# Memory attention and a bilinear layer: seven block products for every quarter from batch 1 on

## The chip, the cores and the metric

The kernel runs on one core of one Trainium2 chip. The metric is the device time of one launch in microseconds (us). Before the change it is 511.87 us, the median of three runs (511.76 to 512.64).

The engines are called as in the profile: PE is the matrix engine (TensorE), DVE is VectorE, ACT is ScalarE, POOL is GpSimd, SP issues the DMAs.

## What is computed

```python
# per batch and head: seq 576, head_dim 64, 32 memories; 8 batches, 8 heads
a = softmax of phi over the sequence
k_m, v_m = a^T k, a^T v                    # 32 x 64 each
attn = softmax(q k_m^T / 8)                # 576 x 32
x = attn v_m                               # all heads side by side: 576 x 512 per batch
# then a layer on x
a, b = x @ w1, x @ w2                      # 512 -> 1024 each
out = ((a * b) @ w3) @ w_out               # 1024 -> 1024 -> 512
```

All is fp32. Nothing between `v_m` and `a * b` is non-linear, so the kernel multiplies `v_m` with w1 and w2 first (a matrix M per batch, 256 x 2048) and then the softmax with M. `w3 @ w_out` is formed once.

## The kernel before

**Numbers.** A matrix is split into a high part, rounded to a short fp32 form (fp32r), and a low part, the rest. A product is three matmuls: high x high, high x low, low x high. Every such matmul has 288 columns, half of a batch's 576 tokens.

**A batch** has three parts.

1. The attention: softmax of phi, the memories (L236, L245), the scores (L285), the second softmax on DVE and ACT, and M in four quarters. A quarter of M (token `M`, L381) is written by PE into two PSUM banks; its high part is a copy on ACT (`Mh`, L392), its low part a subtraction on DVE (`Ml`, L400).
2. a and b. In batches 0 and 1 all four quarters are made *plainly*: `ab_unit` takes 12 matmuls (L655) for 128 features of a and b and half of the tokens, ACT copies a out of PSUM (L664), DVE multiplies it with b (L667). That is 16 units, 192 matmuls a batch. From batch 2 on two of the four quarters are made plainly (96 matmuls) and two by *seven block products* instead of eight (Winograd's form of Strassen's scheme), `block_product` (L695), 6 matmuls each, 84 for the two.
3. The output, also by seven block products (`out_unit`, L782): GpSimd forms sums of g = a * b (L733, L744, L746, L748), ACT and DVE split the operands (`h`, L760; `l`, L766), PE takes 14 units of 12 matmuls, ACT and DVE combine (L799, L807, L815), SP stores.

**Block products of a quarter.** The operands are sums of M's blocks and of the softmax's quarters. Of M: ACT copies one block out of PSUM (`Mr`, L409), DVE forms three sums (`Ms`, L412), ACT rounds them (`Mt`, L420), DVE forms the low parts (`Mu`, L424). Of the softmax: four sums on DVE (`T`, L342) with high and low parts (`Th`, `Tl`, L353). The seven products meet in three pairs of banks, alpha, beta and gamma. ACT copies three intermediate states out of PSUM (L707), DVE adds the banks to them (L717), in six instructions a quarter, and multiplies four times (L727).

**PSUM** is eight banks: four under ab (lent by number), two under o, two under x.

**Order.** Every engine executes its instructions in the order in which a list of tokens emits them: `FIRST` for batch 0, `SECOND` for batch 1, `BATCH` for the rest. A sign says which batch a token is for: `-` the current one, none the next one, `+` the one after. `P1` is a block product, `k`, `e`, `v` its copies, sums and multiplications, `O` an output unit, `f` and `S` GpSimd's sums, `C1` to `C5` the conversion of the float64 weights at the start, `W` the product w3 @ w_out, `K`, `D`, `E`, `F` and the like its splitting, `Q` a difference of weight columns that block products need (L906, DVE).

Of the kernel before, what the change touches and what calls it, by code (L numbers as in the profile page):

```python
# [37 lines left out]
"""
SECOND = """
-mu1 A A tok1 a -tr1 g -M2 a -M3 A -ah1 -Mh3 -Mh2 a A Q -al1 g g a g -Ml3 phi1 A A top a g bm a bs g kv1 exp A A  # L40
phi2 -Ml2 Q f0 a be mem g A norm memc block a h0 g A a tok2 blockc +top M1 a g sc0 +exp g scc0 M0 mx0 A A Mh1 l0 kv2
a f2 g a f1 sb0 ex0 f3 Ml1 A sm0 a Mh0 A g a A g Ml0 +bm g A +norm O mu0 +bs a h1 h2 l1 h3 a l3 l2 tr0 +be sc1 M2
+mem g g M3 Mr Ms O Mh2 S2 S3 scc1 Mt Ml2 mx1 h4 +memc O Mu S1 l4 h6 p1 h5 l5 l6 S4 Mr O O ah0 h8 O h7 Ms u2 C11 l7
O +block h13 h9 l8 sb1 Mt O ex1 h10 Mh3 l9 Mu l10 al0 O p5 O l13 h11 l11 O sm1 O h12 q2 C22 l12 mu1 tr1 Ml3 O
+blockc ah1 O C21 al1 C12
"""
BATCH = """
A A a a g A g a g -T1 h0 phi2 tok2 -T3 A -T2 a g A l0 a -T4 g +top A A -Th1 +bm -Th0 h1 a g +exp A -Tl0 M0 +bs a a
sc0 M1 f0 -Tl1 g Mh0 g Mh1 scc0 Ml0 P1 k10 Ml1 mx0 kvx2 k11 P5 P6 k51 k50 P2 sb0 k20 P3 e10 k21 +be P5 e11 ex0 e20
v1 k50 e21 P7 P1 f2 k51 e40 v2 e41 sm0 k11 v4 k10 P4 l1 P3 P6 P2 e30 v3 k20 e20 k21 f1 f3 e21 P7 mu0 h2 e40 v2 e41 O  # L50
e11 e10 P4 v4 v1 e30 v3 M2 sc1 M3 h3 l2 l3 kvy2 Mh2 Mr +mem Ms S2 +norm h4 +memc O Ml2 S3 p1 l4 h5 Mt tr0 O S1 O h6
S4 scc1 l5 Mu ah0 h8 O l6 Mr h7 O mx1 u2 O l7 C11 h10 O l8 h9 Ms h11 l9 O p5 O l10 l11 h12 sb1 O +block al0 Mt h13
l12 C22 l13 ex1 Mh3 sm1 O Mu mu1 Ml3 +blockc q2 O tr1 ah1 C12 O C21 al1
"""

# [6 lines left out]
def memory_attention__then__bilinear_ffn_kernel(  # L62
# [39 lines left out]
    ps_ab = ctx.enter_context(tc.tile_pool(name="ps_ab", bufs=1, space=bass.MemoryType.PSUM))  # L102
    ps_ox = ctx.enter_context(tc.tile_pool(name="ps_ox", bufs=1, space=bass.MemoryType.PSUM))
# [5 lines left out]
    NQ = 4  # L109
    FQ = DF // NQ  # L110
# [8 lines left out]
    class Banks(list):  # L119
        slots = ()  # L120

        def done(self, i):
            if self.slots:
                free_banks.append(self.slots[i])

    free_banks = [0, 1, 2, 3]

    def pair_ab(n=2):
        slots = [free_banks.pop(0) for _ in range(n)]
        banks = Banks(ps_ab.tile([P, 512], F32, name="ab", tag=f"ab{s}") for s in slots)  # L130
        banks.slots = slots
        return banks

    def pair_o(n=2):
        o = ps_ox.tile([P, 2, 512], F32, name="o")
        return Banks([o[:, i] for i in range(2)] + [o])

    def pair_x(n=2):
        x = ps_ox.tile([P, 2, 512], F32, name="x")
        return Banks([x[:, i] for i in range(2)] + [x])  # L140

    def both(banks):
        return [(slice(0, 2), banks[2])] if banks[2:] else [(slice(i, i + 1), x.unsqueeze(1)) for i, x in enumerate(banks)]
# [41 lines left out]
    ready, beside = {}, {}  # L185

    def attention(b):
# [20 lines left out]
        def spread_max(bank):  # L208
            v["mxb"] = bank(1)
            ps = v["mxb"][0][:, : NT * P]  # L210
            for t in range(NT):
                nc.tensor.transpose(ps[:, t * P : (t + 1) * P], v["mx"][:, t : t + 1].broadcast_to([P, P]), ident)

        def sub_max():
# [8 lines left out]
            v["mxb"].done(0)  # L223
# [4 lines left out]
        def memories(bank):  # L228
            kvt = loaded.pop(("kv", b))
            ps = v["memories"] = bank()  # L230
            if b - 1 in beside:
                ps = v["memories"] = Banks(x[:, HALF : HALF + 2 * D] for x in ps[:2])
# [30 lines left out]
        def blocks(bank):  # L263
            v["blocks"] = bank(1)
            ps = v["blocks"][0][:, : NT * P]
            for t in range(NT):
                nc.tensor.transpose(ps[:, t * P : (t + 1) * P], v["kvm"][:, t], ident)

        def spread():
            ps = v["blocks"][0][:, : NT * P]  # L270
            p4 = ps.rearrange("p (t g m) -> p t g m", t=NT, m=M)
            for t, (ko, vo) in enumerate(((0, D), (D, 0))):
                nc.vector.tensor_scalar_mul(km[b % 2][ko : ko + D], p4[ko : ko + D, t], scale)
                nc.vector.tensor_copy(out=vm[b % 2][vo : vo + D], in_=p4[vo : vo + D, t])
            v["blocks"].done(0)

        def scores(n, bank):
# [3 lines left out]
            banks = v["scores", n] = bank()  # L281
# [21 lines left out]
        def soft_max(n):  # L303
            st = v["st", n] = att.tile([P, NBLK, 1], F32, name=f"st{n}")
            nc.vector.tensor_reduce(out=st, in_=v["s"][:, n], axis=AX.X, op=ALU.max)
# [9 lines left out]
        def soft_sum(n):  # L315
            ss = v["ss", n] = att.tile([P, NBLK, 1], F32, name=f"ss{n}")
# [8 lines left out]
        def probs(n):  # L325
            if n == 0:
                v["at"] = att.tile([P, 2, S], F32, name="at")
            nc.vector.transpose(out=v["at"][:, n], in_=v["s"][:, n].rearrange("p k m -> p (k m)"))

        def probs_high(n):  # L330
            if ("A", b) not in ready:
                ready["A", b] = [att.tile([P, 2, S], F32R, name=x, tag=x) for x in ("ah", "al")]
            nc.scalar.copy(out=ready["A", b][0][:, n], in_=v["at"][:, n])

        def probs_low(n):
            hi, lo = (x[:, n] for x in ready["A", b])
            nc.vector.tensor_tensor(out=lo, in0=v["at"][:, n], in1=hi.bitcast(F32), op=ALU.subtract)

        def prob_sums(i):
            (x11, x21), (x12, x22) = [[v["at"][:, n, t * HALF : (t + 1) * HALF] for t in range(NT)] for n in range(2)]  # L340
            out, in0, in1 = {1: (x11, x12, x11), 3: (x12, x22, x12), 2: (x22, x22, x11), 4: (x21, x21, x22)}[i]
            nc.vector.tensor_tensor(out=out, in0=in0, in1=in1, op=ALU.subtract)  # L342
# [6 lines left out]
        def sums_low(n):  # L349
# [18 lines left out]


    m_tags = (2, 3, 4, 0, 5, 6, 7, 1)  # L370

    def memory_weights(b):
# [3 lines left out]
        def step(q, bank):  # L376
            ps = ms["ps", q] = bank()
# [603 lines left out]
```

## Time and profile before

| | us |
|---|---|
| median of three runs | 511.87 |
| the profiled execution: span from the first to the last instruction | 510.1 |
| PE busy | 500.6 |
| DVE busy | 446.4 |
| ACT busy | 311.5 |
| POOL busy | 147.2 |

What the page gives for the profiled execution's own time is its span; the runs' median stands 1.8 us above it (511.87 - 510.1).

How to read it: the busy time of an engine is the time in which at least one of its instructions runs. Matmuls overlap, so a matmul's own duration is about twice the distance to the next one. DVE's instructions overlap too, by some 0.08 us. The view by stretches gives the busy time of each engine between two times; stretches here are cut where PE starts a batch's a and b (74.06 us for batch 0, then 131.10, 191.91, 245.96, 300.01, 354.07, 408.11, 460.02); PE's last matmul ends near 505.9.

### The profile page before, as it was taken

How to read it: one execution, taken by the hardware profiler on the slowest of the kernel's cores; microseconds unless marked ns; L12 is line 12 of the kernel's file. 1: busy time of each engine (PE TensorE's matmuls, PEld its weight loads, DVE VectorE, ACT ScalarE, POOL GpSimd, SP SyncE). 2: the span in 40 equal slices, each digit the busy share in tenths (PEclk: the TensorE clock that was granted, in tenths of full speed). 3: DMA queues.
4: the chain of work that ended last, by engine and by line, in shares of the span. 5: the costliest groups of instructions: out<-in, count | busy, mean ns of one | idle time of the engine just before them, and what ended most of it. 6: DMA issues, size and time to landing. Idle time of an engine off the chain costs nothing.

```text
span 510.1 us, 11167 instructions
## 1 busy us (share of the span) xinstructions
PE 500.6 (98%) x4416; PEld 434.6 (85%) x4416; DVE 446.4 (88%) x805; ACT 311.5 (61%) x566; POOL 147.2 (29%) x158
## 2 busy tenths in 40 slices
PE   8998999999999999999999999999999999999996
PEld 7344449889889899889988998899898998899996
DVE  4978988888889997999899989999899979997692
ACT  6877889866346655656474747565566555654451
POOL 0003105755020800153023602180108011630480
PEclk9999999999999999999999999999999999999999
DMA  8999943703674047201821064203620230011001
GB/s 282 414 405 350 387 168 110 276 1 118 209 267 154 3 140 243 83 3 41 267 87 73 26 197 161 84 26 128 231 84 3 67 120 1 3 48 48 0 24 69
DMA packets 29795, 68.86 MB, mean 135 GB/s; under 512 B 1840, under 2 KB 10032, under 8 KB 29744
## 3 DMA queue, kind: packets, MB, share of 16 engines
q1 hardware_dynamic: 29744, 68.16, 37.8%
q8 instruction: 34, 0.56, 0.5%
q14 instruction: 17, 0.14, 0.1%
HBM read 58.72 MB, written 9.44 MB: 134 GB/s over the span
## 4 chain that ended last, share of the span: by engine, by line
PE 89%; DMA 7%; ACT 1%; DVE 1%; SPq 1%; issue 0%; ACTq 0%
PE ab L655 25%; PE o L782 19%; PE x L782 11%; PE ab L695 9%; PE ab L782 5%; DMA kv<-in_kv 4%; PE ab L381 3%; PE x L236 3%; DMA raw<-in_w_out 2%; PE o L557 2%; PE x L557 2%; PE x L695 2%; PE o L695 2%; PE o L381 1%; PE x L381 1%; PE ab L285 1%
## 5 line engine op out<-in xcount | busy, mean ns | idle before, releaser
L655 PE MATMUL ab<-ah,mh 128*128 128x288 f32 x320 | 95.8, 300 | 0.0
L655 PE MATMUL ab<-al,mh 128*128 128x288 f32 x320 | 94.4, 295 | 0.0
L655 PE MATMUL ab<-ah,ml 128*128 128x288 f32 x320 | 94.4, 295 | 0.0
L760 ACT CAST sh<-g 128x576 fp32r<-128x576 f32 x98 | 65.7, 676 | 34.6 <-PE x L782 8.5
L766 DVE TENSOR_TENSOR sl<-g,sh 128x576 fp32r<-128x576 f32 x98 | 82.2, 855 | 3.2 <-ACT sh L760 2.6
L733 POOL TENSOR_TENSOR g<-g,g 128x288 f32<-128x288 f32 x32 | 26.2, 838 | 201.0 <-DVE g L667 196.5
L782 PE MATMUL o<-sh,Wh 128*128 128x288 f32 x248 | 73.6, 297 | 0.0
L782 PE MATMUL o<-sh,Wl 128*128 128x288 f32 x248 | 73.2, 295 | 0.0
L782 PE MATMUL o<-sl,Wh 128*128 128x288 f32 x248 | 73.1, 295 | 0.0
L655 PEld LDWEIGHTS ab<-ah,mh 128*128 128x128 f32 x320 | 60.2, 188 | 4.2 <-DVE g L667 1.7
L655 PEld LDWEIGHTS ab<-al,mh 128*128 128x128 f32 x320 | 60.2, 188 | 0.2 <-issue 0.2
L655 PEld LDWEIGHTS ab<-ah,ml 128*128 128x128 f32 x320 | 60.2, 188 | 0.0
L664 ACT COPY a_sb<-ab 128x288 f32<-128x288 f32 x80 | 31.4, 399 | 33.9 <-PE ab L655 33.0
L667 DVE TENSOR_TENSOR g<-ab,a_sb 128x288 f32<-128x288 f32 x80 | 35.6, 453 | 18.4 <-PE ab L655 13.7
L744 POOL TENSOR_TENSOR q<-g,g 128x288 f32<-128x288 f32 x28 | 23.0, 849 | 93.2 <-ACT mh L392 69.2
L782 PEld LDWEIGHTS o<-sh,Wh 128*128 128x128 f32 x248 | 46.6, 188 | 2.9 <-issue 2.5
L782 PEld LDWEIGHTS o<-sh,Wl 128*128 128x128 f32 x248 | 46.6, 188 | 0.0
L782 PEld LDWEIGHTS o<-sl,Wh 128*128 128x128 f32 x248 | 46.6, 188 | 0.0
L782 PE MATMUL x<-sh,Wh 128*128 128x288 f32 x136 | 40.4, 297 | 0.0
L782 PE MATMUL x<-sh,Wl 128*128 128x288 f32 x136 | 40.1, 295 | 0.0
L782 PE MATMUL x<-sl,Wh 128*128 128x288 f32 x136 | 40.1, 295 | 0.0
L748 POOL TENSOR_TENSOR g<-g,q 128x288 f32<-128x288 f32 x28 | 34.7, 1267 | 0.0
(194 smaller groups left out, 1277.3 us busy)
## 6 DMA issues: line engine op xcount, KB each, us to landing
kv<-in_kv SPq DMA_DIRECT2D x16, 1024.0 KB, 8.5
q<-in_qT SPq DMA_DIRECT2D x8, 1152.0 KB, 5.4
outT<-c SPq DMA_DIRECT2D x31, 288.0 KB, 2.2
raw<-in_w3T SPq DMA_DIRECT2D x6, 1024.0 KB, 11.2
ph<-in_phiT SPq DMA_DIRECT2D x8, 576.0 KB, 4.7
a<-in_phi_tok SPq DMA_DIRECT2D x8, 576.0 KB, 6.1
raw<-in_w SPq DMA_DIRECT2D x4, 1024.0 KB, 15.7
kv<-in_w SPq DMA_DIRECT2D x3, 1024.0 KB, 14.3
```

What stands on the lines that cost most here:

```text
L381: nc.tensor.matmul(ps[t][g * M : (g + 1) * M], lhsT=vm[b % 2][d, g], rhs=w12_sb[q][d, :, g], start=True, stop=True,)
L557: nc.tensor.matmul(pw[r][i][:, cols], lhsT=x[:, i * P : (i + 1) * P], rhs=wos[k // half][:, k % half, cols], start=k == 0 and cols.start == 0,
L655: nc.tensor.matmul(banks[w][:, :HALF], lhsT=x[:, t, w, fc : fc + P], rhs=y[:, n, t * HALF : (t + 1) * HALF], start=i == 0, stop=i == len(t ...
L664: nc.scalar.copy(out=a_sb, in_=banks[0][:, :HALF])
L667: nc.vector.tensor_tensor(out=G[n, f // half][:, f % half], in0=banks[1][:, :HALF], in1=a_sb, op=ALU.mult)
L695: nc.tensor.matmul(G[bank, q][w][:, :HALF], lhsT=xs[x][:, w], rhs=ys[y], start=i in (1, 2, 5) and k == 0, stop=i in (2, 3, 4) and k == 2, ...
L733: nc.gpsimd.tensor_tensor(out=low, in0=top, in1=low, op=ALU.subtract)
L744: gp(out=s2, in0=a22, in1=s3, op=ALU.subtract)
L748: gp(out=a12, in0=a12, in1=s2, op=ALU.subtract)
L760: nc.scalar.copy(out=hi, in_=src)
L766: nc.vector.tensor_tensor(out=lo, in0=src, in1=hi.bitcast(F32), op=ALU.subtract)
L782: nc.tensor.matmul(ps[j][:, :HALF], lhsT=piece(x, s, 2 * part + k)[:, jc], rhs=y[:, k], start=i in first and part == 0 and k == 0 and t == ...
```

## The change

- **a and b.** Batch 0 stays plain. From batch 1 on all four quarters are made by seven block products: 168 matmuls a batch.
- **P1.** Its result is no longer copied out to SBUF and added back by DVE. ACT copies it from alpha into the bank in which P2 is to be accumulated (token `s`, `seed`), and P2 adds to it there. So are p1 of the output (`keep`) and P2's unit, whose result ACT then copies out (`C11`).
- **M.** High, low and sum parts of the quarters rotate through three slots (`slot`) in place of one place for each quarter; a fourth quarter's `M`, `Mr`, `Ms`, `Mh`, `Mt`, `Ml`, `Mu` stand at the start of the next batch's list (`-M3` and so on). All four quarters need `Mr`, `Ms`, `Mt`, `Mu`, and the difference `Q` is taken for all four.
- **The softmax's parts.** For batches without plain quarters one of the four quarter-blocks of `ah` and `al` is left out (`probs_high`, `probs_low`). The sums `T` move from the start of the batch that uses them to the end of the list before it.
- **km and vm** (the blocks of the memories) are copied out of PSUM by ACT (`spread`), not by DVE.
- **PSUM** is one pool of four pairs of banks, lent side by side (`Pair`).
- **Lists.** All are new, with one more, `LAST`, for batch 7. GpSimd's sums are single tokens now (`Sa0` to `Sc3`), where one token was a row of them.

```diff
+PLAIN = [(0, 1, 2, 3)] + [()] * (B - 1)
+    class Pair:
+        def __init__(self, n=2, full=True, seeded=False):
+            self.slots, self.banks = [], []
+            for side in range(n):
+                slot = next(i for i in free_banks[side] if not seeded or (side, i) in written)
+                free_banks[side].remove(slot)
+                (written.add if full else written.discard)((side, slot))
+                self.slots.append(slot)
+                self.banks.append(psum.tile([P, 512], F32, name="ps", tag=f"ps{side}{slot}"))
...
             for t, (ko, vo) in enumerate(((0, D), (D, 0))):
-                nc.vector.tensor_scalar_mul(km[b % 2][ko : ko + D], p4[ko : ko + D, t], scale)
-                nc.vector.tensor_copy(out=vm[b % 2][vo : vo + D], in_=p4[vo : vo + D, t])
+                nc.scalar.activation(out=km[b % 2][ko : ko + D], in_=p4[ko : ko + D, t], func=AF.Copy, scale=scale)
+                nc.scalar.copy(out=vm[b % 2][vo : vo + D], in_=p4[vo : vo + D, t])
...
+        def slot(q):
+            return (NQ * b + q) % 3
+        def read(q):
+            left = ms["left", q] = ms.get(("left", q), 1 if q in PLAIN[b] else 2) - 1
+            if left == 0:
+                ms["ps", q].done()
...
-        if i in (1, 2, 5):
-            G[bank, q] = pair_x() if i == 2 else pair_o() if i == 5 and q == NQ - 1 else pair_ab()
+        if i in (1, 5):
+            G[bank, q] = Pair()
...
-                    start=i in (1, 2, 5) and k == 0,
+                    start=i in (1, 5) and k == 0,
...
+    def seed(q, w, G):
+        if ("beta", q) not in G:
+            G["beta", q] = Pair(seeded=True)
+        for (_, out), (_, x) in zip(G["beta", q].parts(w), G["alpha", q].parts(w)):
+            nc.scalar.copy(out=out, in_=x)
...
-        bank, kept = {1: ("beta", 1), 2: ("gamma", 2), 4: ("alpha", 5)}[i]
+        bank, kept = {2: ("gamma", 2), 4: ("alpha", 5)}[i]
...
     def keep(what, G):
+        if what == "p1":
+            G["beta"] = Pair(seeded=True)
+            for (_, out), (_, x) in zip(G["beta"].parts(), G["alpha"].parts()):
+                nc.scalar.copy(out=out, in_=x)
+            return
...
-            units = [ab_unit(b, n, f, G) for fs in parts for n in range(2) for f in fs]
-            for what in tokens((FIRST, SECOND, BATCH)[min(b, 2)]):
+            for what in tokens(LISTS[min(b, 2) if b < B - 1 else 3]):
```

Three places in the engines' orders. In their rows g00, g10, g01 and g11 are the four parts of g, sl a low part, sh a high part, ml and ms the low parts of M and of its sums, c a copied bank, at the softmax and its sums.

DVE where batch 2 ends and batch 3 begins, before: from the last result of batch 2 to the first plain units.

```order
L815 TENSOR_TENSOR c_2805<-x_2807,c_2805 128x576
L337 TENSOR_TENSOR al_2770<-at_2726,ah_2769 128x576
L667 TENSOR_TENSOR g00_2973<-ab_2978,a_sb_3005 128x288
L667 TENSOR_TENSOR g00_2973<-ab_2992,a_sb_3007 128x288
L667 TENSOR_TENSOR g00_2973<-ab_3011,a_sb_3025 128x288
L342 TENSOR_TENSOR at_2726<-at_2726 128x288 x3
L667 TENSOR_TENSOR g00_2973<-ab_3037,a_sb_3051 128x288
L766 TENSOR_TENSOR sl_3068<-g00_2973,sh_3029 128x576
```

DVE at the same place after: the low parts for batch 3 stand ahead of its first multiplication, and sums of M and of the banks behind it.

```order
L383 TENSOR_TENSOR sl_3089<-at_2870,sh_3063 128x576
L383 TENSOR_TENSOR sl_3091<-at_2870,sh_3044 128x576
L427 TENSOR_TENSOR ml_3093<-ps_2860,mh_3026 128x512
L427 TENSOR_TENSOR ml_3093<-ps_2861,mh_3026 128x512
L455 TENSOR_TENSOR ms_3068<-tmp_3048,ms_3068 128x768
L711 TENSOR_TENSOR g00_3097<-ps_3110,a_sb_3129 128x288
L445 TENSOR_TENSOR tmp_3131<-ps_3113,tmp_3131 128x256
L445 TENSOR_TENSOR tmp_3131<-ps_3112,tmp_3131 128x256
L752 TENSOR_TENSOR c_3154<-ps_3135,c_3154 128x288
L752 TENSOR_TENSOR c_3154<-ps_3136,c_3154 128x288
```

The multiplications of plain units gave way to sums out of PSUM, and low parts of the next batch's operands moved to the batch's border.

DVE in batch 2 while GpSimd makes its sums S, before: low parts of operands (two inputs in SBUF), one after the other.

```order
L766 TENSOR_TENSOR sl_2766<-q_2647,sh_2722 128x576
L424 TENSOR_TENSOR ms_2724<-q_2647,ms_2724 128x768
L766 TENSOR_TENSOR sl_2786<-g00_2224,sh_2758 128x576
L305 TENSOR_REDUCE st1_2803<-s_sb_2430 128x18
L766 TENSOR_TENSOR sl_2820<-g00_2224,sh_2789 128x576
L815 TENSOR_TENSOR c_2718<-ab_2728,c_2718 128x288
```

DVE in the same part of batch 2 after, from the last multiplication that S waits for.

```order
L711 TENSOR_TENSOR g11_2316<-c_2623 128x288
L797 TENSOR_TENSOR sl_2794<-g01_2314,sh_2775 128x576
L427 TENSOR_TENSOR ml_2812<-ps_2777,mh_2809 128x512
L427 TENSOR_TENSOR ml_2812<-ps_2778,mh_2809 128x512
L445 TENSOR_TENSOR tmp_2816<-ps_2778,tmp_2816 128x256
L445 TENSOR_TENSOR tmp_2816<-ps_2777,tmp_2816 128x256
L797 TENSOR_TENSOR sl_2837<-g00_2313,sh_2835 128x576
L333 TENSOR_REDUCE ss1_2856<-s_sb_2493 128x18
```

Instructions that read PSUM, and reductions, now stand between the low parts there.

POOL from batch 5 to batch 6, before: rows of four.

```order
L744 TENSOR_TENSOR q_4894<-g11_4474,g10_4473 128x288 x4
L746 TENSOR_TENSOR g00_4471<-q_4894,g00_4471 128x288 x4
L748 TENSOR_TENSOR g01_4472<-g01_4472,q_4894 128x288 x4
L733 TENSOR_TENSOR g10_5222<-g00_5220,g10_5222 128x288 x4
L744 TENSOR_TENSOR q_5620<-g11_5223,g10_5222 128x288 x4
```

POOL in batch 5 after.

```order
L768 TENSOR_TENSOR g10_4667<-g00_4665,g10_4667 128x288 x4
L779 TENSOR_TENSOR q_4990<-g11_4668,g10_4667 128x288 x2
L781 TENSOR_TENSOR g00_4665<-q_4990,g00_4665 128x288 x2
L783 TENSOR_TENSOR g01_4666<-g01_4666,q_4990 128x288
L779 TENSOR_TENSOR q_4990<-g11_4668,g10_4667 128x288
```

The same sixteen sums a batch are there, the last twelve of them interleaved.

## Rows read from the trace of the kernel before

**Rows 1.** The page, part 1: busy time of each engine.
```profile
span 510.1 us, 11167 instructions
PE 500.6 (98%) x4416; PEld 434.6 (85%) x4416; DVE 446.4 (88%) x805; ACT 311.5 (61%) x566; POOL 147.2 (29%) x158
```

**Rows 2.** The page, part 4: the chain that ended last, by engine.
```profile
PE 89%; DMA 7%; ACT 1%; DVE 1%; SPq 1%; issue 0%; ACTq 0%
```

**Rows 3.** Stretches: length, then busy us (instructions) of PE, PEld, DVE, ACT, POOL.
```profile
0.00:74.06 74.06, 69.05 (x316) 34.51 (x317) 58.70 (x97) 58.18 (x76) 7.68 (x14) 1.00 0.91 334
74.06:131.10 57.04, 56.99 (x544) 51.75 (x543) 50.49 (x87) 41.40 (x74) 30.32 (x32) 1.00 0.38 135
131.10:191.91 60.81, 60.81 (x658) 54.42 (x658) 55.93 (x99) 34.62 (x65) 14.78 (x16) 1.00 0.44 156
191.91:245.96 54.05, 54.05 (x530) 50.09 (x530) 50.17 (x95) 31.40 (x62) 15.41 (x16) 1.00 0.28 93
...
354.07:408.11 54.04, 54.04 (x530) 50.08 (x530) 50.91 (x96) 31.78 (x63) 15.40 (x16) 1.00 0.33 111
408.11:460.02 51.91, 51.52 (x447) 47.79 (x446) 46.28 (x89) 28.76 (x56) 16.02 (x16) 1.00 0.12 42
460.02:505.90 45.88, 45.88 (x348) 45.81 (x347) 32.07 (x56) 21.08 (x43) 16.76 (x16) 1.00 0.10 33
```

**Rows 4.** The chain piece by piece, batch 4: start, us, engine, line, matmuls.
```profile
300.01 11.11 PE ab L655 x84
...
334.80 3.18 PE ab L782 x24
```

**Rows 5.** Groups on DVE: count, busy us, mean ns, idle before.
```profile
L766 DVE TENSOR_TENSOR sl<-g,sh 128x576 fp32r<-128x576 f32 x98 | 82.2, 855 | 3.2 <-ACT sh L760 2.6
L412 DVE TENSOR_TENSOR q<-ab,q 128x256 f32<-128x256 f32 x36 | 14.1, 418 | 2.8 <-ACT q L409 2.4
L424 DVE TENSOR_TENSOR ms<-q,ms 128x768 fp32r<-128x768 f32 x6 | 9.2, 1531 | 0.0
L424 DVE TENSOR_TENSOR msl<-q,msh 128x768 fp32r<-128x768 f32 x6 | 5.4, 904 | 0.0
L273 DVE TENSOR_SCALAR km<-ab 64x128 f32<-64x128 f32 x12 | 3.4, 280 | 1.6 <-PE ab L267 1.6
L906 DVE TENSOR_TENSOR w<-w 64x1024 f32<-64x1024 f32 x2 | 2.4, 1222 | 0.1
```

**Rows 6.** Timeline of DVE in batch 4: start, us, line, what, count.
```profile
305.25 1.44 DVE L342 TENSOR_TENSOR at<-at 128x288 f32<-128x288 f32 x3
...
310.08 0.75 DVE L353 TENSOR_TENSOR sl<-at,sh 128x576 fp32r<-128x576 f32 x1
...
319.10 0.81 DVE L717 TENSOR_TENSOR c<-x,c 128x288 f32<-128x288 f32 x2
319.83 0.45 DVE L717 TENSOR_TENSOR c<-ab,c 128x288 f32<-128x288 f32 x1
...
336.81 1.54 DVE L424 TENSOR_TENSOR ms<-q,ms 128x768 fp32r<-128x768 f32 x1
338.28 1.37 DVE L766 TENSOR_TENSOR sl<-g,sh 128x576 fp32r<-128x576 f32 x1
...
340.24 0.75 DVE L766 TENSOR_TENSOR sl<-g,sh 128x576 fp32r<-128x576 f32 x1
...
342.98 1.20 DVE L412 TENSOR_TENSOR q<-ab,q 128x256 f32<-128x256 f32 x3
```

**Rows 7.** Timeline of POOL over the same time.
```profile
333.38 4.16 POOL L746 TENSOR_TENSOR g<-q,g 128x288 f32<-128x288 f32 x4
337.50 4.93 POOL L748 TENSOR_TENSOR g<-g,q 128x288 f32<-128x288 f32 x4
```

**Rows 8.** Groups on ACT: copies of a bank out of PSUM.
```profile
L707 ACT COPY c<-ab 128x288 f32<-128x288 f32 x60 | 21.1, 408 | 11.7 <-PE ab L695 10.3 <-DVE c L717 0.8
L409 ACT COPY q<-ab 128x256 f32<-128x256 f32 x12 | 4.5, 375 | 1.7 <-PE ab L381 1.4 <-DVE ms L424 0.3
```

More of the change, by code (lines that the diff above doesn't have):

```diff
@@ L182, in load @@
             LOADS[what](b)
-    ready, beside = {}, {}
+    ready = {}
     def attention(b):
@@ new lines, in probs_high @@
+            if n == 1 and NA == 3 and PLAIN[b]:
+                extra = [big.tile([P, 2, HALF], F32R, name=x, tag=x, bufs=4)[:, :1] for x in ("sh", "sl")]
+                v["parts", 1] = [(0, extra, slice(0, 1)), (1, v["ahl"], slice(2, 3))]
+            elif n == 1 and not PLAIN[b]:
+                v["parts", 1] = [(1, v["ahl"], slice(2, 3))]
+            else:
+                v["parts", n] = [(0, v["ahl"], slice(2 * n, 2 * n + 2))]
+            for t, (hi, lo), x in v["parts", n]:
+                w = x.stop - x.start
+                src = v["at"][:, n].rearrange("p (t s) -> p t s", t=NT)[:, t : t + w]
+                nc.scalar.copy(out=hi[:, x], in_=src)
+                for i in range(w):
+                    ready["A", b][n, t + i] = hi[:, x.start + i], lo[:, x.start + i]
@@ L553, in product @@
         if k == 0 and r not in pw:
-            pw[r] = Banks(pair_o()[:2] + pair_x()[:2]) if r else pair_ab(4)
+            pairs = [Pair(), Pair()]
+            pw[r] = [(pairs[i // 2], i % 2) for i in range(4)]
         x = w3s[f"w3{r}", k // 2][:, k % 2]
@@ new lines, in block_keep, with block_result @@
+    def block_keep(i, q, w, G):
+        if ("kept", i, q) not in G:
+            G["kept", i, q] = big.tile([P, 2, HALF], F32, name="c", tag="c", bufs=NC)
+        for j, x in G["gamma" if i == 5 else "alpha", q].parts(w):
+            nc.scalar.copy(out=G["kept", i, q][:, j], in_=x)
+    def block_result(i, q, w, G):
+        bank, kept = {2: ("gamma", 2), 4: ("alpha", 5)}[i]
+        for j, x in G[bank, q].parts(w):
+            c = G["kept", kept, q][:, j]
+            nc.vector.tensor_tensor(out=c, in0=x, in1=c, op=ALU.add)
+            if i == 2:
+                G[bank, q].done(j)
@@ L796, in keep @@
     def keep(what, G):
-        c = G[what] = big.tile([P, 2, HALF], F32, name="c", tag="c", bufs=3)
-        for j, x in both(G["o" if what in ("p1", "u2") else "x"]):
-            nc.scalar.copy(out=c[:, j], in_=x[:, :, :HALF])
+        if what == "p1":
[3 more added lines that the diff above has]
+            return
+        bank = G[{"u2": "alpha", "p5": "gamma", "p4": "delta"}[what]]
@@ L835, in memory_bank @@
-    def memory_bank(b, in_a, what):
-        if what[0] == "-" or b == 0 and in_a:
-            return pair_ab if b == 0 else pair_x if what[-1] == "3" else pair_o
-        return (pair_x if what[-1] == "1" else pair_o) if in_a else pair_ab
+        halves = b == B - 1 and what == "C21"
+        c = G[kept] if kept in G else big.tile([P, 2, HALF], F32, name="c", tag="c", bufs=NC)
+        for j, x in G[bank].parts():
+            if kept in G:
+                nc.vector.tensor_tensor(out=c[:, j], in0=x, in1=c[:, j], op=ALU.add)
+            else:
+                nc.scalar.copy(out=c[:, j], in_=x)
+            if halves:
+                store(b, n, oh, c, slice(j, j + 1))
```

497 lines of the change are left out of this document (230 added, 267 removed).

## The prediction, made before the changed kernel ran

> **What bounds the kernel now.** First the busy times: PE is busy for 500.6 of 510.1 us, DVE for 446.4 [rows 1]. Then the chain that ended last: 89% of it is PE, 1% DVE [rows 2]. Then the stretches: in every batch from 131 us on PE is busy for the whole stretch (54.05 of 54.05 us in the first of the four equal batches 2 to 5, 54.04 of 54.04 in the last), while DVE is busy for 50.2 to 50.9 of it and ACT for some 31.6 [rows 3]. So PE sets the time, and DVE is only 3.1 us a batch behind it. That small distance is what this change has to be read by: whatever takes work off PE shows in the time only until DVE becomes the later one.
>
> **What PE saves.** 84 matmuls took 11.11 us, so one counts 0.132 us in a row of them [rows 4]. Batch 1 drops from 192 to 168 matmuls for a and b, batches 2 to 7 from 180 to 168: 24 + 6 x 12 = 96 matmuls, 12.7 us. Nothing else on PE changes in number. If PE stayed the bound everywhere, the span would be 510.1 - 12.7 = 497.4, and a batch of 54.05 would take 52.46.
>
> **What DVE gets, batches 2 to 5.** Behind another instruction one costs less than its row: two L717 take 0.81 and one 0.45, so 0.36 each further one; three L412 take 1.20, so 0.40 each; a low part of 768 takes 0.90 alone, so 0.82 queued [rows 5, 6]. Per batch, against before:
> - two more quarters need M's sums: 6 x 0.40 = +2.4, and their low parts 2 x 0.82 = +1.6;
> - bank additions: four quarters x 4 in place of two x 6, so 4 more: +1.4. The multiplications are 16 as before;
> - km and vm go to ACT: four of 0.28, queued about 0.25: -1.0;
> - one quarter-block less in `al`: -0.3; results, with C11 now on ACT: -0.6; the low parts of M in eight pieces: +0.1.
>
> The sum is +3.6: DVE's 50.9 becomes 54.5 us a batch, where PE needs 52.46. **The order of the two turns round**, and 54.5 is above the 54.05 that a batch takes now. At the batch's border the order shows how tight it is: two low parts of the softmax's sums, M's low part and its sums' low part (3.3 us of DVE) stand between PE's last output unit and DVE's first multiplication of the next batch, and the third block product there needs them.
>
> **Batches 0 and 1.** They pay most: batch 0 has to prepare batch 1's block products and keeps its own plain work. Counted over both lists from the first a/b unit on, DVE gets 15 more sums of M (6.0), 5 more low parts of them (4.1), 16 bank additions (5.8), 8 sums T at 1.44/3 = 0.48 (3.8), 4 low parts of these at 0.75 - 0.08 (2.7), one more `Q` (1.2); it loses 12 km/vm (-3.0), result work (-1.8) and part of `al` (-0.3): +18.5. Its 50.5 + 55.9 = 106.4 us [rows 3] become 124.9. PE's 117.85 become 114.7. Batch 6 prepares batch 7 and takes over its T as well: +4.4, so 46.3 becomes 50.7 against PE's 51.9 - 1.6 = 50.3. Batch 7 itself has 32 us of DVE work in 45.9 us [rows 3]: there PE's -1.6 counts.
>
> **What part of DVE's time is collision.** While POOL worked without a break from 333.4 to 342.4, a low part that takes 0.75 a little later took 1.37, one of M's 1.54 where its like takes 0.90 [rows 5 to 7]; three of them in that batch lost 1.9 us together. Over the kernel L766's mean is 0.855 against 0.75: 10 us. Instructions that read PSUM, such as L412, took the same with and without POOL. So of the 54.5 some 1.9 are collision, and of the 124.9 some 4. After the change POOL's twelve sums S are interleaved and DVE has PSUM reads and reductions between the low parts. Whether that takes the collisions away I can't read from the old trace: bounds are 0 and the old 1.9 (or a little more, since two more low parts a batch can be hit). I take half, as the order now has about as many low parts near S as PSUM reads.
>
> By the Trainium skill, *SBUF — State Buffer*, section "Who interferes with whom", a VectorE instruction with both inputs in SBUF and a GpSimd instruction that reads SBUF take a shared read interface in turns, and the one that starts first holds it for its whole length. The rows agree: the low parts and M's sums, with two SBUF inputs, are the ones that grew (1.37 against 0.75). By that rule alone POOL, which here becomes ready when a DVE instruction ends and the next DVE instruction starts at once, would mostly be the one that waits, and the time would be rival B's, 507.7.
>
> **ACT, PSUM and SP.** ACT gets the seeds, more copies and km/vm: per batch 10 copies of 0.41, two of 0.375, two roundings and the results, some 9 us on 31.8 [rows 3, 8]; at 41 of 54 it isn't the bound. A seed writes PSUM, which no row shows: between nothing and twice 0.41 a quarter, and PE has one other product or M's matmuls to do in between, so I take it at 0; without that cover it is 0.8 x 4 = 3.3 a batch on PE, inside what DVE's lateness covers anyway. The loads keep their number; SP issues them some us of PE work ahead of their first reader and the DMA share of a batch is 0.33 or less [rows 3], so 0. The start up to 74 us has the same products and conversions in another order: 0, give or take 2.
>
> **The sum, likeliest case (A): DVE is the bound from batch 0 to 6.** Half of the collisions stay, DVE idles for 0.7 us a batch (2 in batches 0 and 1).
> - Batches 0 and 1: 124.9 - 2 + 2 = 124.9 against 117.85: +7.0.
> - Batches 2 to 5: 54.5 - 0.9 + 0.7 = 54.3 against 54.05: 4 x 0.25 = +1.0.
> - Batch 6: 50.7 - 0.8 + 0.9 = 50.8 against 51.9: -1.1.
> - Batch 7: -1.6 and 0.5 of start: -1.1.
>
> Together +5.8: a span of 515.9, and with the 1.8 between span and median **517.7 us**. Its own range is 511 to 525 (collisions all gone in batches 0 and 1 alone, or all kept and twice the idle time).
>
> **Rivals.**
> - **B, PE stays the bound from batch 2 on** (faster). Collisions go, because POOL's sums now fall beside PSUM reads. Then batches 0 and 1 take 124.9 - 4 + 1 = 121.9 (+4.0), batches 2 to 5 52.8 (4 x -1.25 = -5.0), batches 6 and 7 -1.6 each: -4.2, so 507.7. For it: the order just shown. Against it: DVE would have to run at 99.6%.
> - **C, the two wait for each other in turn** (slower by much). A quarter holds three of the four pairs of banks while M's last quarter holds the fourth, so PE's next product waits for a multiplication or addition on DVE, and DVE then waits for that product. It decides from the point where DVE idles as long as before beside its larger work: 54.5 + 3.1 = 57.6 a batch (+14.2), batches 0 and 1 124.9 + 5.7 (+12.7), batch 6 +1.6: +28.5, so 540. Half of that is as likely as all.
> - **D, the change brings just what PE saves**: -12.7, so 499.2. DVE's busy time would have to overlap with itself more than its rows show.
>
> **How the numbers follow.** A 0.54, B 0.27, C 0.13, D 0.06. A run can tell about 0.2% (1 us) from no change. Faster than 510.8 are D and nearly all of B: 0.33. Between 510.8 and 512.9 lie the edges of A and B: 0.08. Slower: 0.59. The range leaves out D and the far end of C: 503 to 532. The likeliest case alone: 511 to 525.
>
> **What would show it.** In the profile after: PE busy near 488, in stretches no longer whole, with idle time that ends on DVE; DVE busy near 475 to 483 and above 98% of each stretch of batches 2 to 5; batches 0 and 1 longer than 117.85. The group of low parts (L797 there) tells the collisions: a mean near 0.75 speaks for B, near 0.85 for A. PE still whole in each stretch would prove the turn-round wrong; DVE idle of 3 us a batch beside waits of PE for DVE would be C.

## The result, and the profile after

The changed kernel takes 516.45 us (median of six runs, 515.27 to 518.57), the kernel before 511.88 in the same comparison: a ratio of 1.0094, 95% interval 1.0072 to 1.0117. It is slower by about 0.9%. The forecast was 517.7. The profiled execution is one of the longer ones, 518.16 us with a span of 516.1; the runs of 516.17, 518.16 and 518.57 us have a mean granted clock of 0.996, those of 515.27, 515.64 and 516.74 one of 0.999. Terms are compared by spans, 516.1 against 510.1: +6.0, which is 1.4 more than the medians differ by.

The page of the changed kernel, parts 1 and 4 (beside [rows 1, 2]): busy time of each engine, and the chain that ended last.

```profile
PE 501.9 (97%) x4320; PEld 424.3 (82%) x4320; DVE 472.6 (92%) x901; ACT 367.9 (71%) x770; POOL 141.1 (27%) x158
...
PE 63%; DVE 20%; DMA 9%; ACT 4%; issue 3%; SPq 1%; DVEq 0%; ACTq 0%
```

DVE's share of the chain went from 1% to 20%. The chain shows the place: batches 2 to 4 begin with block products on PE and end with a row of DVE pieces beside the output. In batches 5 and 6 it stays on PE to their end: the two engines are close. PE has 96 matmuls fewer, but its busy time is 1.3 us longer. Part of that is waiting that is counted as busy (a row below, 1.39 us in place of 1.02), part a lower clock, part dearer matmuls.

The changed kernel by stretches, cut as in [rows 3] (length, then busy us of PE, PEld, DVE, ACT, POOL, granted clock, DMA share, GB/s):

```profile
0.00:74.68 74.68, 69.62 (x317) 34.10 (x317) 59.82 (x96) 61.16 (x84) 8.67 (x15) 1.00 0.91 338
74.68:134.48 59.80, 59.07 (x560) 52.24 (x559) 58.38 (x104) 45.78 (x92) 29.62 (x31) 1.00 0.35 119
134.48:197.45 62.97, 59.21 (x603) 52.47 (x602) 58.79 (x119) 43.12 (x101) 13.25 (x16) 0.97 0.46 156
197.45:252.39 54.94, 53.93 (x518) 48.56 (x518) 52.45 (x106) 39.07 (x89) 14.73 (x16) 1.00 0.30 104
252.39:306.50 54.11, 54.01 (x518) 48.61 (x518) 53.12 (x108) 38.74 (x90) 14.74 (x16) 1.00 0.32 110
306.50:360.59 54.09, 53.98 (x519) 48.61 (x518) 53.15 (x108) 38.73 (x90) 14.72 (x16) 1.00 0.32 111
360.59:414.86 54.27, 54.17 (x519) 48.68 (x518) 53.15 (x108) 38.80 (x90) 14.72 (x16) 1.00 0.32 110
414.86:466.62 51.76, 51.68 (x435) 46.36 (x434) 49.39 (x101) 35.14 (x79) 14.85 (x16) 1.00 0.07 24
```

The 6.0 us lie there: start +0.6, batches 0 and 1 +4.9 (122.77 against 117.85), batches 2 to 5 +1.2 (217.41 against 216.2), batch 6 -0.15, batch 7 with the end -0.6 (49.5 against 50.1).

**A wait that the prediction had at nothing.** Batch 1 takes 62.97 us though DVE is busy for only 58.79. The timeline of SP's queue where batch 0 ends (start, us, engine, line, what, count):

```profile
128.01 7.82 SPq L824 DMA_DIRECT2D outT<-c  x4
135.88 0.46 SPq L167 DMA_DIRECT2D ph<-in_phiT  x1
137.91 0.35 SPq L172 DMA_DIRECT2D a<-in_phi_tok  x1
138.32 0.94 SPq L180 DMA_DIRECT2D kv<-in_kv  x2
139.30 1.37 SPq L188 DMA_DIRECT2D kv<-in_kv  x2
```

The timeline of PE a little later, with idle time and what ended it in brackets:

```profile
149.62 3.54 PE L252 MATMUL ps<-kv,a 128*32 128x128 f32 x64 [2.19 <-DMA kv<-in_kv]
```

And that of DVE:

```profile
151.68 1.35 DVE L212 TENSOR_REDUCE mx<-ph 128x2 f32<-128x1152 f32 x1 [1.95 <-DMA ph<-in_phiT]
```

SP takes its DMAs in order. It stands behind batch 0's four stores until 135.88, so batch 2's k and v are issued at 138.32 and land some 10.7 us later: PE waits 2.19 us. Phi for batch 3, issued behind them, keeps DVE waiting for 1.95. In batches 2 to 5 too phi stands behind the stores, and the reduction over it waits 0.3 to 1.6 us. The wait for k and v depends on how soon they land: in the run below with five multiplications on GpSimd they stand at the same place in the queue, landed 9.5 us after their issue, and PE waited less, and for DVE:

```profile
147.62 1.96 PE L252 MATMUL ps<-kv,a 128*32 128x128 f32 x64 [0.97 <-DVE sm L224]
```

### The profile page after: what moved, and what is told of

It reads as the page before. It is cut to its first block, busy times and chain, and to the rows that moved or that the text cites. A ratio compares the mean times of both kernels' runs of the same rounds, so it can differ in the third digit from the quotient of the medians.

```text
span 516.1 us, 11286 instructions
## 1 busy us (share of the span) xinstructions
PE 501.9 (97%) x4320; PEld 424.3 (82%) x4320; DVE 472.6 (92%) x901; ACT 367.9 (71%) x770; POOL 141.1 (27%) x158
## 4 chain that ended last, share of the span: by engine, by line
PE 63%; DVE 20%; DMA 9%; ACT 4%; issue 3%; SPq 1%; DVEq 0%; ACTq 0%
PE ps L727 27%; PE ps L812 19%; DMA kv<-in_kv 6%; DVE sl L797 5%; PE ps L409 4%; PE ps L590 4%; DMA raw<-in_w3T 3%; PE ps L252 3%; PE ps L697 2%; DVE tmp L445 2%; PE ps L301 2%; DVE ml L427 1%; DVE c L846 1%; DVE at L372 1%; DVE at L344 1%
## 5 line engine op out<-in xcount | busy, mean ns | idle before, releaser
L812 PE MATMUL ps<-sh,Wh 128*128 128x288 f32 x448 | 134.2, 299 | 0.2 <-ACT ps L830 0.2
L812 PE MATMUL ps<-sl,Wh 128*128 128x288 f32 x448 | 132.2, 295 | 0.3 <-DVE sl L797 0.3
L812 PE MATMUL ps<-sh,Wl 128*128 128x288 f32 x448 | 132.2, 295 | 0.0
L812 PEld LDWEIGHTS ps<-sh,Wh 128*128 128x128 f32 x448 | 84.0, 187 | 10.5 <-issue 7.5
L812 PEld LDWEIGHTS ps<-sl,Wh 128*128 128x128 f32 x448 | 84.3, 188 | 0.7 <-DVE sl L797 0.5
L812 PEld LDWEIGHTS ps<-sh,Wl 128*128 128x128 f32 x448 | 84.1, 188 | 0.0
L590 PE MATMUL ps<-wo,w 128*128 128x512 f32 (+1 forms) x132 | 57.2, 585 | 2.1 <-DVE wo L578 2.1
L727 PE MATMUL ps<-sh,ms 128*128 128x288 f32 x224 | 53.0, 303 | 2.3 <-ACT ps L740 1.2
L752 DVE TENSOR_TENSOR c<-ps,c 128x288 f32<-128x288 f32 x112 | 44.4, 448 | 4.1 <-ACT c L746 2.6
L427 DVE TENSOR_TENSOR ml<-ps,mh 128x512 fp32r<-128x512 f32 x64 | 40.7, 677 | 0.6
```

The source lines that it names most:

```text
L427: nc.vector.tensor_tensor(out=ml[:, t], in0=x, in1=ms[q][0][:, t].bitcast(F32), op=ALU.subtract)
L590: nc.tensor.matmul(pw[r][i][0][pw[r][i][1]][:, cols], lhsT=x[:, i * P : (i + 1) * P], rhs=wos[k // half][:, k % half, cols], start=k == 0 ...
L727: nc.tensor.matmul(G[bank, q][w][:, :HALF], lhsT=xs[x][:, w], rhs=ys[y], start=i in (1, 5) and k == 0, stop=i in (2, 3, 4) and k == 2, ski ...
L752: nc.vector.tensor_tensor(out=c, in0=x, in1=c, op=ALU.add)
L812: nc.tensor.matmul(ps[j][:, :HALF], lhsT=piece(x, s, 2 * part + k)[:, jc], rhs=y[:, k], start=i in first and part == 0 and k == 0 and t == ...
```

## Experiments

Theory A is the prediction's likeliest case: DVE's work sets the time of batches 0 to 6. B says that PE still does, C that they wait for each other in turn. Ratios are to the kernel before, measured on the same chip beside each group of runs (511.75 to 512.08).

**km and vm back on DVE.**

```diff
-nc.scalar.activation(out=km[b % 2][ko : ko + D], in_=p4[ko : ko + D, t], func=AF.Copy, scale=scale)
-nc.scalar.copy(out=vm[b % 2][vo : vo + D], in_=p4[vo : vo + D, t])
+nc.vector.tensor_scalar_mul(km[b % 2][ko : ko + D], p4[ko : ko + D, t], scale)
+nc.vector.tensor_copy(out=vm[b % 2][vo : vo + D], in_=p4[vo : vo + D, t])
```

> The changed kernel with one part undone: km and vm are copied out of PSUM by DVE again, four instructions of some 0.25 us queued, in the lists of batches 0 to 6. Theory A (DVE's work sets the time of batches 0 to 6): 7 x 1.0 = 7 us more, some 523.5 in place of 516.45, less if DVE's idle time of about 1 us a batch takes some of it. Theory B (PE sets the time there, DVE is only nearly as long): no change, 516.5, since ACT is the engine that is relieved and it is not the bound. Theory C (the two wait for each other in turn): about half, 520.

523.61 us, ratio 1.0230 (1.0198 to 1.0262): 7.2 us more than the changed kernel, as A says. The stretch of batch 3, and a wait of PE (us in total, times, longest):

```profile
255.62:310.60 54.98, 54.10 (x518) 48.55 (x518) 53.87 (x111) 38.20 (x86) 14.71 (x16) 1.00 0.31 109
```

```profile
PE ps L409 <- DVE vm L290: 3.5, 4, 0.9
```

In batches 3 and 4 DVE got 0.75 us and the batch grew by 0.87. Batch 0 grew by 2.2, batches 2 and 5 by 1.2 each; batch 6, whose list holds none of these copies, did not grow (51.23 against 51.76). This run alone doesn't separate DVE's work from its order: M's matmuls stand right behind the copies and wait 0.85 to 0.89 us for them in each of batches 2 to 5, as much as batches 3 and 4 grew. The next runs help to tell.

**The same edit in the kernel before, the other way round** (km and vm from DVE to ACT, nothing else).

> The kernel before with one part of the change alone: km and vm copied out of PSUM by ACT in place of DVE, so DVE has 1.0 us less in batches 0 to 6. The counterpart of the run that put them back on DVE in the changed kernel and cost 7.1 us. Theory A (PE sets the time of the kernel before, DVE that of the changed one): no change, 511 to 513. Rival: DVE sets part of the time in the kernel before as well: up to 7 us less, 505.

514.0 us, ratio 1.0025 (0.9998 to 1.0052): no gain. A steady stretch of it:

```profile
301.34:355.39 54.05, 54.05 (x531) 50.09 (x530) 49.98 (x94) 32.75 (x67) 15.40 (x16) 1.00 0.32 110
```

DVE has 0.9 us less than in [rows 3], PE is whole, and the length is the same 54.05. So the same four instructions a batch are worth nothing before the change and 7 us after it.

**A third of the output's matmuls left out.**

```diff
-for t, (x, y) in enumerate(((Wh, hi), (Wl, hi), (Wh, lo))):
+for t, (x, y) in enumerate(((Wh, hi), (Wh, lo))):
```

> The changed kernel without the matmuls high part of the data x low part of the weights in the output's block products (one of three; that term is left out of the result): 56 matmuls of 0.132 us a batch, 7.4 us of PE a batch, with nothing taken from DVE. Theory A: batch 7, where DVE is not the bound, gets shorter by up to 7; each of batches 1 to 6 by no more than DVE's idle time in it (1 us in the steady ones, 4 in batch 1), so 500 to 507. Theory B: 8 x 7.4 = 59 us less, 457.

508.71 us, ratio 0.9918 (0.9889 to 0.9947). The stretch of batch 3:

```profile
248.13:301.82 53.69, 49.04 (x463) 41.48 (x462) 52.63 (x107) 38.35 (x89) 14.74 (x16) 1.00 0.32 111
```

PE lost 56 matmuls a batch, 7.4 us of work (its busy time fell by 4.9, since it now waits for DVE). Batch 2 lost 0.8, batch 3 0.4, batch 4 0.8, batches 0, 5 and 6 nothing (they took 0.15 to 0.25 more), and batch 7, where DVE isn't the bound, lost 4.1. Batch 1 lost 3.8, no more than it loses in the next run by its loads alone. B's 457 is out. DVE alone needs 53.3 to 54.4 us in each of batches 2 to 5 with its short waits.

**Batch 2's k and v loaded earlier.**

```diff
 FIRST:  ... mem memc A11 a11 l40 y0 a33 f2 w1 block
+kv2
 SECOND: ... c11 v11 f0
-kv1
```

> The changed kernel with one load moved: k and v of batch 2 are loaded in batch 0's list, behind batch 1's own memories, in place of batch 1's list, where the issue on SP stands behind batch 0's stores. In the profile PE waited 2.2 us for that load and DVE 1.95 us for the phi load queued behind it. If these two waits are on the path: 2 to 4 us less, some 513.5, and the stretch of batch 1 gets shorter by that. If batch 1 is bound by DVE's work whatever PE does (4.1 us idle there could be filled later): no change, 516.5.

512.77 us, ratio 1.0003 (0.9977 to 1.0029): 3.7 us less, and no longer slower than the kernel before by anything that these runs can tell. Batch 1 takes 59.14 in place of 62.97, the other batches what they took, within 0.4. The memories of batch 2 on PE, with no wait before them:

```profile
146.80 1.95 PE L252 MATMUL ps<-kv,a 128*32 128x128 f32 x64
```

More than the wait of 2.19 came back; the section on the hardware says why.

**Five multiplications a batch on GpSimd** (`v20 v40 v21 v41 v22` become `V20 ...` in SECOND and BATCH).

> The changed kernel with five of the eight multiplications a batch whose inputs both lie in SBUF (quarters 0 and 1, and one of quarter 2) made by GpSimd in batches 1 to 6: 5 x 0.37 = 1.85 us less of DVE a batch. Theory A: batches 1 to 6 get shorter until PE's own work of about 53.0 us is reached, 1.1 us each, 1.9 in batch 1: some 509. Theory B: no change, 516.5. A rival on the way: GpSimd's five more instructions lengthen DVE's instructions with SBUF inputs that run beside them, by up to 0.4 us each, so the gain goes and the time stays at 515 to 517 with a higher mean of the low parts.

511.95 us, ratio 1.0008 (0.9981 to 1.0034): 4.5 us less. Batches 2 to 5 take 53.55 to 53.64, 0.5 to 1.4 less, with PE whole; batch 6 takes 51.18 (0.6 less), PE whole too. Batch 1 takes 59.99, 3.0 less, but in this execution PE also had no wait for k and v there (the row above), so its 3.0 are not DVE's work alone. DVE's low parts have the same mean as without it, 793 ns, but the low part of M's sums is hit more often (a mean of 1038 against 945).

**Both together, and a third of the output's matmuls left out of that.**

> The changed kernel with both, the earlier load of k and v and five multiplications a batch on GpSimd. Each alone shortened batch 1 most (by 3.8 and 3.0 us), the second also batches 2 to 6 (0.5 to 1.4 each). If the two gains are of different causes (a DMA wait, DVE's work): they add up, 516.45 - 3.7 - 4.5 = 508.3. If they are the same lateness of batch 1 taken away twice: only one counts there, 511.5.

> The kernel of both parts, without the matmuls high part of the data x low part of the weights in the output (56 a batch, 7.4 us of PE; that term is left out of the result). It tells what sets 53.57 us a batch in batches 2 to 5 with five multiplications on GpSimd. If it is PE now (its floor is 53.5, not the 52.5 that the prediction took): they fall by 1.5 to 1.9 each, to DVE's own 51.7 to 52, so some 12 to 14 us less than with both parts alone, 4 of it in batch 7. If it is still DVE: only batch 7 gets shorter, 4 to 5 us.

Both together: 511.84 us, ratio 0.9987 (0.9968 to 1.0006). The gains did not add up: batch 1 takes 58.99, only 0.15 less than with the loads alone, so there it was one lateness taken away twice, the second case of the expectation. A wait of DVE in this kernel (us in total, times, longest):

```profile
DVE mx L212 <- DMA ph<-in_phiT: 5.6, 5, 1.9
```

Batches 2 and 5 took 54.2 and 54.6, and there the reduction waited 1.5 and 1.85 us for phi. With fewer matmuls: 502.76 (two runs), ratio 0.9806 (0.9749 to 0.9863), a span 8.9 us shorter. Batch 7 gave 4.1 of it, batches 2 to 5 from 0.6 to 1.2 each, down to 52.7 in two of them. So PE did set the 53.57; the expected 51.7 to 52 wasn't reached, since DVE is busy for 51.4 and still waits 1.3.

**Differences of the weight columns on GpSimd** (`Q1 Q2 Q3` of batch 0, on top of both).

> The kernel of both parts, and three of batch 0's four differences of weight columns (Q, 1.22 us each on DVE) made by GpSimd. Theory A for batch 0 (DVE's work sets its 59.6 us): 3.7 us less than with both parts alone. Rival: GpSimd's three instructions take about twice as long, run beside DVE's low parts and stand ahead of the sums of g on its own queue, so the gain goes: no change, or 1 to 2 us more.

513.05 us, ratio 1.0005 (0.9985 to 1.0025): the rival. Batch 0:

```profile
74.18:135.88 61.70, 59.50 (x560) 52.16 (x559) 58.28 (x101) 45.83 (x92) 38.02 (x34) 1.00 0.43 154
```

3.7 us of work left DVE, and its busy time in batch 0 is 58.28 where it was 58.38 in the changed kernel. GpSimd's three took 3.4, 2.4 and 2.8 us, and DVE's instructions in batch 0 grew by 3.5: the low parts by 1.2 (five were hit where it had been two), the addition of 1e-9 (L223) and a weight conversion (L578) by 0.9 each, a subtraction (L325) by 0.5.

**Phi's load ahead of the stores.**

```diff
 FIRST:  ... l70 M2 tr0 l71 tr1
+phi2
 SECOND:
-phi1
 ... O71 tr1
+phi3
 BATCH:  ... P50 k502
-phi2
 ... l30 tr1
+phi3
```

> The changed kernel with the earlier load of k and v and with phi's load moved too: from the head of each batch's list, where its issue on SP stands behind the stores of the batch before and DVE's reduction over phi waited for it (0.3 to 1.6 us a batch, 5.0 in all), to the place where its buffer comes free, ahead of those stores. If that wait of DVE is on the path: 0.3 to 1.5 us less in each of batches 2 to 5, some 510 to 511 in place of 512.77, and no wait of the reduction for a DMA from batch 1 on. If DVE's idle time there is made up by PE's work anyway: no change, 512.8.

> The same with five multiplications a batch on GpSimd. With the loads of k and v alone the two gains did not add up: batches 2 and 5 took 54.2 and 54.6 us instead of 53.57, and in both DVE's reduction had waited 1.5 and 1.9 us for phi. If that wait ate the gain: batches 2 to 5 take 53.5 each, batch 1 some 58.5, 508 to 509.5 in all, under the 511.9 of the kernel before. If not: 511.8 as with both parts.

> The same, and batch 0's four sums T of the softmax's quarters made by GpSimd (1.8 us less of DVE in batch 0). Theory A for batch 0: its 59.6 us get 1 to 1.8 us shorter. Rival: GpSimd makes them one after the other at about 1 us each at the end of the batch, where the block products of batch 1 wait for their high and low parts: no change, or 1 us more.

With both loads moved: 513.78 us, ratio 1.0015 (0.9990 to 1.0040), its ten runs 511.67 to 515.55, so the median tells nothing against the 512.77 without phi's move. Its profile does: no wait of the reduction for phi, batches 2 to 5 at 53.4 to 53.9 instead of 53.95 to 54.9. With five multiplications on GpSimd too: 510.36, ratio 0.9959 (0.9936 to 0.9982), batches 2 to 5 at 53.57 or 53.58 each. The sums T on GpSimd: 510.64, ratio 0.9973 (0.9953 to 0.9992), batch 0 at 62.2 us against 60.8, longer, not shorter.

But batch 0 had become 1.2 us longer by phi's early load itself. The timeline of ACT there (five multiplications on GpSimd, both loads moved):

```profile
131.27 0.70 ACT L835 COPY c<-ps 128x288 f32<-128x288 f32 x2 [2.29 <-DMA outT<-c]
```

ACT waited for a store to give back a buffer `c`; the store ran behind the load that had been put ahead of it.

**Phi's first load put back** (`phi1` at the head of SECOND, no `phi2` in FIRST).

> The kernel with both loads moved and five multiplications on GpSimd, but phi's load for batch 2 stands at the head of batch 1's list again. With that load ahead of batch 0's stores batch 0 had become 1.2 us longer (60.83 against 59.64): ACT waited 2.3 us for a store to give back a buffer c, and the store's transfer ran behind the load's. If that is the cause: batch 0 takes 59.6 again with batch 1 at 58.5 to 59.0 and 53.57 in batches 2 to 5, about 1 us less than with the load ahead, a span of 507.5 and a median of 509.3. If batch 0 was longer for another reason: no change, 510.4.

509.81 us, ratio 0.9961 (0.9947 to 0.9975), the fastest of all and faster than both kernels. Batches 0, 1, 2 and 4:

```profile
74.34:134.13 59.79, 59.01 (x560) 52.16 (x559) 58.42 (x104) 45.80 (x92) 29.60 (x31) 1.00 0.44 159
134.13:193.10 58.97, 57.56 (x603) 51.04 (x602) 56.98 (x114) 43.30 (x101) 18.06 (x21) 1.00 0.40 136
193.10:246.67 53.57, 53.57 (x519) 48.49 (x518) 51.47 (x102) 39.30 (x90) 17.88 (x21) 1.00 0.31 106
300.24:353.81 53.57, 53.57 (x518) 48.49 (x518) 51.67 (x102) 38.56 (x91) 17.90 (x21) 1.00 0.32 111
```

Batch 0 is back at 59.8 (59.6 by the cut of the expectations, 0.16 earlier), and PE is whole again in batches 2 to 5.

## Why the prediction came out

**The size is luck in good part.** The forecast had +7.0 us in batches 0 and 1, all of it DVE's work, and loads at 0. Measured are +4.9, and 3.8 of these are the k and v load and what came with it; with that load moved, batches 0 and 1 cost 1.1 more than before, and the whole kernel is level with the one before (512.77, ratio 1.0003). So the slowdown that was forecast for one reason came in the main for another, a term that I had put at nothing.

**The turn-round (A) is shown for batches 2 to 5, and it is narrow.** Taking 7.4 us of work a batch from PE gives 0.8 at most there (batch 5 gives nothing). Taking 1.1 to 1.7 us of busy time from DVE gives 0.5 to 1.4, until PE is whole at 53.57. In the kernel before, less DVE work gives nothing. Batch 0 speaks for A as well: it grew by 2.2 with the copies on DVE and lost nothing with the matmuls left out (though 3.4 us of it ran at the lower clock then). In batches 1 and 6 the two engines are even. With the loads moved, five multiplications fewer on DVE change batch 1 from 58.65 to 58.50 and batch 6 from 51.62 to 51.17, and with the matmuls left out they take 59.1 and 52.0. C had DVE idle for 3 us a batch; it is idle for 0.9 to 1.1 in batches 3 to 5.

**The sign that I had named would have misled.** "PE still whole in each stretch would prove the turn-round wrong": PE is busy for 53.98 of 54.09 and DVE turned out the bound all the same; PE's 488 and DVE's 475 to 483 us of busy time came out as 501.9 and 472.6. The step that failed here is PE's floor of 52.46. It is 53.57, as the chain of waits of the fastest version shows in its batch 4, where nothing but PE stands (start, us, what):

```profile
300.24 0.80 PE ps L727 x6
301.04 1.02 PE ps L409 x16
302.06 9.76 PE ps L727 x72
311.82 0.22 PE ps L230 x2
312.04 0.65 PE ps L301 x16
312.68 7.37 PE ps L727 x54
320.06 0.73 PE ps L301 x16
320.79 5.07 PE ps L727 x36
...
332.17 0.37 PE ps L283 x2
```

168 matmuls of block products take 23.0 us (0.80 + 9.76 + 7.37 + 5.07), 0.137 each; I had priced all at the plain 0.132 of [rows 4]. In the kernel before they already were the dearer ones, 11.5 us for 84. Its chain of waits in batch 4, with the score matmuls (L285) and the first block products (L695):

```profile
313.96 0.48 PE ab L285 x16
...
315.30 2.58 PE ab L695 x18
```

That makes 0.4 us a batch: 96 plain ones at 0.132 gave way to 84 at 0.137, a saving of 1.2 and not 1.6. The two groups of score matmuls take 0.65 and 0.73 where one took 0.48 beside M's matmuls, 0.4 more; the transposes of the blocks 0.15; the rest, 0.1 to 0.2, is in the output. So DVE's work with its waits passes PE by only 0.5 us (DVE's busy time, 53.15, lies even below PE's 53.57), and a wait of that size hides in PE's busy time: in batch 4 of the changed kernel, where the group of M's matmuls at the border has to wait for banks that hold the last results (start, us, what):

```profile
307.42 1.39 PE ps L409 x16
```

against 1.02 above.

**Batches 2 to 5: +1.0 forecast, +1.2 measured.** DVE's busy time was to be 53.6; it is 53.1 in three of them and 52.45 in batch 2. Idle time was to be 0.7; it is 1.0, and 2.5 in batch 2 with its wait of 1.6 for phi.

**Batches 0 and 1: +7.0 forecast, +4.9 measured, by two errors that partly cancel.** DVE's busy time was to rise from 106.4 to 122.9; it rose to 117.2 (58.38 + 58.79). By groups of the trace the sums of M, the bank additions and T came out within 0.6 us of the count. What it missed: one quarter of M now crosses into batch 2 with its low parts (M's take 10.7 us in place of 12.4, and their sums' low parts 1.2 less than counted); one weight conversion more stands before 74 us, and weight conversions take 2.0 less in the two batches; a low part of T crosses too (0.7). On the other side idle time is 5.6 us instead of 2, 4.2 of it in batch 1, most of that by the DMA waits: "SP issues them some us of PE work ahead of their first reader, so 0" was wrong by 3.8 us in this execution (2.2 of waiting and 1.6 at a lower clock), as the run with the earlier load shows.

**Batches 6 and 7: -2.7 forecast (-2.2 with 0.5 for the start), -0.75 measured (the start took 0.6).** In batch 6 PE's floor is again higher than I took (51.17 in the fastest version, PE whole). Batch 7 got the fourth quarter of its own M, 1.0 us of PE that stood in batch 6 before. I had counted that quarter as going out of a batch and coming in from the one before; batch 7 has nobody to hand it on to.

**Collisions: rather more than the half that I took stayed, in part at another place.** The groups on DVE (beside [rows 5]: count, busy us, mean ns):

```profile
L797 DVE TENSOR_TENSOR sl<-g,sh 128x576 fp32r<-128x576 f32 x98 | 76.5, 793 | 3.4 <-ACT sh L791 3.3
L455 DVE TENSOR_TENSOR ms<-tmp,ms 128x768 fp32r<-128x768 f32 x28 | 26.5, 945 | 0.0
L334 DVE TENSOR_SCALAR ss<-ss 128x18 f32<-128x18 f32 x16 | 8.6, 535 | 0.5
```

The low parts' mean fell from 855 to 793; the low part of M's sums had taken 1531 in six cases and 904 in six, and takes 945 on the mean now. The mean of 793 lies between the two signs named, 0.75 for B and 0.85 for A. In a steady batch low parts lose 0.5 us where they and M's sums together lost 2.0, but L334 loses 0.8 that it didn't lose before: 1.3 of 2.0. The one low part that is hit in batch 4, on DVE (start, us, what):

```profile
342.00 1.25 DVE L797 TENSOR_TENSOR sl<-g,sh 128x576 fp32r<-128x576 f32 x1
343.17 0.74 DVE L333 TENSOR_REDUCE ss<-s_sb 128x18 f32<-128x576 f32 x1
343.95 0.76 DVE L334 TENSOR_SCALAR ss<-ss 128x18 f32<-128x18 f32 x1
```

And on POOL at that time:

```profile
341.83 0.81 POOL L783 TENSOR_TENSOR g<-g,q 128x288 f32<-128x288 f32 x1
342.59 2.08 POOL L781 TENSOR_TENSOR g<-q,g 128x288 f32<-128x288 f32 x2
```

GpSimd's sum began at 341.83, the low part at 342.00, and the low part ended about 0.6 us after that sum: the one that had begun first held the other up, which is the rule of the Trainium skill, *SBUF — State Buffer*, "Who interferes with whom". Here GpSimd began first, so the rule did not lead to B. The reduction L333 kept its 0.74. The addition of 1e-9 to 18 numbers a row (L334) took 0.76 and ended just after GpSimd's two sums; it took 0.18 in each of its 16 places in the kernel before, where a sum ran beside only one of them. The same section lists tensor_scalar among the operations that can take both port pairs; the row agrees.

**Seeds cost PE nothing in batches 2 to 5.** In the fastest version PE is whole there with all seeds in it, and its extra 1.1 us a batch is named above without them: 0, of the range 0 to 3.3, stands. In batch 1 the 0 was wrong: PE waits 1.2 us for the first seed (until 137.77 us; 1.0 to 1.2 in every trace of the changed kernel and its variants), which stands on ACT behind a rounding of M's sums that itself waited 1.18 for DVE. ACT, at 38.7 to 39 of 54, isn't the bound; forecast was 41.

## What to carry to other kernels

When work moves from the engine that is the bound to one that is 3 us behind, ask for both floors, with each kind of instruction at its own price, before you say which is later. A total that comes out right doesn't vouch for its terms: compare them stretch by stretch. A busy share near 100% doesn't prove a bound when two engines are within 1% of each other; adding a little work to each, or taking much away, does. Loads that stand behind stores in one in-order queue are late by however late the stores are: issue them where their buffer comes free, unless a store then holds up a buffer that is needed sooner.

## What the runs showed of the hardware that was not expected

**A wait of PE can cost more than its length.** The granted clock of the changed kernel around the wait for k and v:

```profile
140.00:147.30 7.30, 7.17 (x54) 6.82 (x52) 7.18 (x15) 6.87 (x18) 0.81 (x1) 1.00 1.01 369
147.30:149.60 2.30, 0.13 (x1) 0.01 (x1) 2.27 (x8) 1.78 (x4) 0.00 (x0) 1.00 1.04 229
149.60:153.10 3.50, 3.48 (x66) 3.12 (x66) 1.55 (x3) 0.00 (x0) 0.80 (x1) 0.53 0.18 60
```

PE stood for 2.19 us, and then ran at a granted 0.53, about the lower of its two levels (1.2 GHz of 2.4), for the next 3.5 us: the 64 matmuls of the memories took 3.54 us, where they took 1.95 in the run with the earlier load. 2.19 + 1.59 = 3.8, and that is what batch 1 got back there (62.97 to 59.14). It is not so each time. With km and vm on DVE the same matmuls stood behind a wait of 2.36 us, after 9.54 busy us of 9.90, and the granted clock stayed at 1.00:

```profile
152.26 1.95 PE L252 MATMUL ps<-kv,a 128*32 128x128 f32 x64 [2.36 <-DVE c L752]
```

```profile
152.26:154.20 1.94, 1.94 (x72) 1.74 (x76) 0.29 (x1) 0.00 (x0) 0.80 (x1) 1.00 0.21 74
```

In the run with a third of the output's matmuls left out it fell to 0.51 after a wait of 1.60 us in batch 0. So the length of the wait alone doesn't decide it; what does is open.

**Work handed to GpSimd can come back.** In batch 0 of the run with the differences of weight columns on GpSimd an addition of 1e-9 to two numbers a row on DVE took 1.26 us while GpSimd was at the second of them (95.28 to 97.69); its timeline on DVE:

```profile
96.45 1.26 DVE L223 TENSOR_SCALAR sm<-sm 128x2 f32<-128x2 f32 x1
97.75 0.17 DVE L224 RECIPROCAL sm<-sm 128x2 f32<-128x2 f32 x1
```

A reciprocal of the same two numbers right behind it took 0.17. So 3.7 us of work went off DVE's list and only 0.1 off its busy time. The five multiplications a batch did pay: DVE's busy time fell from 472.6 to 463.4 us.
